# Transposing the attention outputs in the DMA crossbar instead of on TensorE

## The chip, the cores and the metric

The kernel runs on one core of a Trainium2 chip. The metric is the device time of one execution in microseconds. The five engines of the core that matter here are TensorE (PE, with its weight loads listed apart as PEld), VectorE (DVE), ScalarE (ACT), GpSimd (POOL) and SyncE (SP). Each of them works through its own list of instructions in order; they wait for one another on semaphores. Sixteen DMA engines move data; POOL and SP issue the transfers.

## The reference

Four batches of eight heads, 768 rows of 64. Each query row attends to the keys closer than 16 rows and, beside them, to 24 block summaries (the largest key and the mean value of each block of 32). The attention outputs of a batch, heads side by side, are rows of 512 numbers, and these 3072 rows go through two matrix products with a hard-swish between them.

```python
k_sum = k.reshape(B, H, nb, block, D).max(axis=3)
v_sum = v.reshape(B, H, nb, block, D).mean(axis=3)
scores_l = scale * np.matmul(q, k.transpose(0, 1, 3, 2))          # kept where |i - j| < 16
scores_s = scale * np.einsum('bhsd,bhnd->bhsn', q, k_sum) + np.log(block)
a = softmax(concatenate([scores_l_masked, scores_s]))             # over 768 + 24
attn_out = np.matmul(a, np.concatenate([v, v_sum], axis=2))
x = attn_out.transpose(0, 2, 1, 3).reshape(3072, 512)
h = x @ w_in                                                      # 512 x 2048, "GEMM 1"
out = (h * np.clip(h + 3.0, 0.0, 6.0) / 6.0) @ w_out              # 2048 x 512, "GEMM 2"
```

## The kernel before

**Tiling.** A batch has six row tiles T = 0 to 5 of 128 rows each (shifted by 16 rows). Three of them make one token tile: token tile s = 2b for T = 0, 1, 2 of batch b, and s = 2b + 1 for T = 3, 4, 5. There are eight token tiles of 384 rows.

**From attention to GEMM 1.** `scores` (L541) makes the scores on TensorE, ACT takes their exponent (L566) and DVE masks it (L570). `values` (L648) multiplies them with the values on TensorE (L671) into a PSUM pair `S`. `finish` (L687) does the rest for one row tile: DVE takes the reciprocal of the sums (L705) and scales the 128x512 outputs into an SBUF tile `xn` (L709, bf16, rows on partitions). GEMM 1 needs the 512 features on the partitions, so TensorE transposes the tile in four 128x128 matmuls against an identity into a PSUM bank (L724), and ACT or DVE copies the bank into the SBUF tile `x` of the token tile (L726, recorded at the helper's line L463).

**GEMMs.** `f1` (L734) is GEMM 1 for one token tile and 128 of the 2048 inner features: four matmuls of 128x384 (L742), which read all of `x`, then ACT's relu (L747) and DVE's product (L749). The first `f1` of a token tile needs all three of its row tiles. `f2` (L753) is GEMM 2: sixteen matmuls in four groups of four (L762), a copy to an SBUF tile `ot`, and a store issued by SP (L774, two stores L773 and L774 where a tile wraps around).

**Order.** Nothing is scheduled at run time. `ORDER` (L29) is a written list of every operation; each engine executes its operations in the sequence in which their tokens stand there. `F20.0` is the first GEMM 1 product of token tile 2, `G40.5` the store of token tile 4's row tile 0, `v10.3` the fourth operation of `values` for batch 1 beginning at row tile 0, `H2.1` and `H3.0` the halo copies of batches 2 and 3, `u3.4` one of the value-mean copies. A letter after the colon picks the engine of a copy.

**SyncE before the change.** SP issues three kinds of transfer: the stores of `ot`; for batches 2 and 3 the copies of value means into `vaug` (`spread`, L578, 36 KB each, two in a `u` token); and the halos (L437, one of 380 KB in 128-byte pieces, and L439, 32 KB), which copy key-window edges from one set of partitions of `vaug` to another. Eight completion semaphores serve SP's transfers in turn, so one transfer waits for the eighth before it.

**Pools.** There are four `x` tiles, three `xn` tiles, three `ot` tiles, one PSUM bank `o` and two pairs `S`.

The text names only the row tiles of batches 1 to 3; batch 0 is treated apart in the code (`alone`, `banks`).

Of the kernel before, what the change touches and what calls it, by code (L numbers as in the profile page):

```python
# [29 lines left out]
e.1 c.0 K00.0 c.8 z3.0 z1.0 z2.0 K01.0 c.1 Q000.0 K02.0 k00.0 c.2 Q010.0 c.3 c.4 e.0 k00.1 e.3 k00.2:D k00.4 V00.0 V01.0  # L30
k01.0 k01.2:A Q01w2.0 c.6 V02.0 V03.0 q010.0 q000.0 k01.1 k01.4 z0.0 q000.1:A q010.1:A k00.3:A Q01w1.0 I0.0 Q01w0.0 k01.3:A
k03.0 s000.0 k02.0 q030.0 k03.2:A q030.1:D e.2 c.7 I1.0 O0.0 I2.0 q020.0 s010.0 s000.1 s010.1 u00.0 q020.1:A s010.2 k03.1
k02.1 k03.4 k02.4 u00.1:A u00.2:D h010.0:D s000.2 u01.0 s030.0 s030.1 h011.0:D u01.1:D h000.0:D u01.2:D k02.2:A s020.0
s020.1 u02.0 h030.0:D u02.1:D s030.2 h020.0:A s020.2 u03.0 u03.1:D v01.0 v00.0 v00.2 v00.3 v01.2 v01.3 v02.1 I3.0 O2.0 O1.0
v00.1 v01.1 v02.4 v00.4 v00.5 h031.0:A h001.0:A k03.3:A u02.2:A v02.0 v00.6 v00.7:A v01.4 v02.2 v02.3 v01.5 q011.0 v01.6
v02.5 k02.3:A v01.7:D F00.0 v02.6 F00.5 F00.6 q001.0 v02.7:A F00.1 F00.2 q001.1:A F00.3 F00.7 c.5 h021.0:D q031.0 q011.1:A
F00.8 u01.3:D u00.3:D F00.4 F00.9 F01.0 q021.0 F01.3 F01.1 F01.2 q031.1:D F00.15 F00.10 s001.0 q021.1:A F01.4 F01.5 u03.2:D
F00.16 F00.17 s001.1 s001.2 s011.0 F00.11 F00.12 F00.13 F00.14 F01.9 F01.10 c.9 F01.11 F01.6 s011.1 F01.7 s011.2 F01.8
s021.0 F02.9 F02.10 F02.11 s021.1 s021.2 G02.0 s031.0 F02.0 F03.0 F03.3 s031.1 s031.2 F02.1 F03.1 F02.2 F03.2 v04.0 v03.0
v03.1 F03.4 v03.2 F03.5 v04.1 v04.2 F02.3 F02.6 F02.4 F02.5 v03.3 v03.4:A F03.9 v05.0 G02.1 v04.3 z0.1:P z3.1:P K11.0 K12.0  # L40
O3.0 K13.0 z1.1:P K10.0 V12.0 V10.0 V13.0 F03.10 F02.7 v05.1 v05.2 v05.3 v05.4:A F02.8 v04.4:D F03.11 F03.6 F03.7 F10.0
F03.8 F10.3 F10.1 F10.6 F10.4 F10.2 F10.5 F10.9 F10.7 F11.0 F10.8 F10.10 F11.3 F10.11 F11.1 F11.6 F11.2 F11.4 F11.5 F11.7
F11.8 F11.9 F12.6 Q10.0 V11.0 z2.1:P Q12.0 Q13.0 Q11.0 F11.10 F12.7 F11.11 F12.8 F13.0 F12.9 F13.1 F12.10 w12.0 w13.0 F13.2
h121.0:A w11.0 w13.3 w10.0 h100.0:D h130.0:D w10.3 G02.2 F13.6 F13.7 h111.0:D G02.3 F12.0 G02.4:A G01.0 G01.1 G01.2 G01.3
u1.0 h120.0:A F12.1 h101.0:A w10.2:A w13.4:A h131.0:A G01.4:A u1.1:A w12.2:A u1.6:A u1.2:A F12.11 w11.3 F13.8 u1.4:D w11.4:D
w12.3 w10.4:D w12.4:D V22.0 Q20.0 K22.0 K21.0 K20.0 K23.0 Q21.0 Q23.0 Q22.0 V23.0 V21.0 V20.0 w10.1 w10.5:D G00.0 G00.1
F13.9 G00.2 F12.3 G00.3 F13.10 u1.8:A w11.2:A F12.4 h110.0:A w11.1 F12.5 w11.5:D u1.9:D w13.1 w12.1 w12.5:D s100.0 s100.3
s100.1 G00.4:A s110.0 G00.5 s110.1 s110.3 F13.3 G12.0 s120.0 w13.2:A s120.3 s120.1 s110.2 w13.5:D F12.2 F13.11 s110.4 s100.2
# [5 lines left out]
F22.9 F22.10 w21.5:A u2.0 F21.8 w21.3 w21.4:D F22.5 F23.0 Q31.0 Q30.0 V30.0 V32.0 V31.0 V33.0 Q32.0 K33.0 Q33.0 K30.0 K32.0
K31.0 G10.4:A s200.1 u2.1:A F21.9 F21.10 F23.1 F22.11 G11.5 G02.5 u2.2 u2.3 G10.5 H2.0 u2.5 u2.4 w22.1 w22.0 F21.11 F23.3
F23.4 s210.0 G20.0 s210.3 s210.1 F23.2 F23.5 F30.0 G20.1 F23.9 F23.6 w22.5:D F30.1 w22.3 F23.7 w22.4:A F30.2 F23.10 w22.2:D
F23.8 F30.3 G20.2 F30.9 F30.10 s220.0 s220.1 F30.4 s200.2 F23.11 w23.1 F30.11 G20.3 F32.6 F32.0 G20.4:A w23.0 F32.1 w23.5:D
F32.2 F30.5 w23.2:A u3.0 w23.3 s210.2 s220.2 w30.1 G22.0 s220.3 F30.6 G22.1 u3.1:A F32.7 F32.8 w23.4:A F30.7 F30.8 s210.4
s220.4 G22.2 G22.3 G22.4:A s230.0 F31.6 s230.1 s230.3 s230.2 s230.4 F31.3 F31.0 G21.0 F31.4 F31.5 F31.1 v20.0 G21.1 F31.9
F31.10 v20.5 F31.2 v20.1 v20.6 s200.4 F31.11 G21.2 F33.6 F33.7 v20.2 F33.8 F31.7 F31.8 G21.3 F32.9 v20.3 F33.3 G21.4:A  # L60
v20.4:A F33.4 F32.10 u3.4 H2.1 H3.0 G22.5 G20.5 G21.5 v22.0 v25.0 F33.0 w30.0 v22.1 v22.2 F32.11 v25.1 v25.2 F33.1 F33.5
G32.0 F32.3 v20.7 v22.3 F32.4 G32.1 v20.8:A v22.4:A F33.9 F33.2 F32.5 w31.0 F33.10 w30.3 F33.11 F40.0 v23.0 G32.2 F40.9
F40.1 F40.3 w30.4:A F40.10 F40.4 v23.1 F40.2 v23.2 F40.5 F41.3 v23.3 G32.3 v23.4:A F41.4 G32.4:A F40.11 v23.5 F41.5 F40.6
F42.9 G30.0 G30.1 F42.3 v23.6 v23.7 G30.2 w33.0 F42.10 F42.11 w30.5:D w30.2:A F40.7 w31.3 F40.8 w31.2:A F42.4 F42.5 w31.1
F41.0 v25.3 F41.9 F41.1 F41.10 F41.2 F41.11 F42.0 F42.1 w32.1 F42.2 w31.5:D G30.3 F43.6 F43.9 v25.4:A G30.4:A v23.8:D w32.0
w32.3 w33.2:D G31.0 G31.1 w32.4:D F43.7 F43.10 F43.8 w31.4:A s310.0 s310.1 s310.3 G31.2 F43.3 F43.4 w32.5:A F43.5 G31.3
G31.4:A F50.0 F50.1 F42.6 F42.7 F43.11 w32.2:D w33.1 s300.0 s300.3 s300.1 H3.1 G31.5 G32.5 u3.5 u3.3 u3.2 G30.5 F41.6 G41.0
F41.7 F42.8 F50.2 s310.2 F41.8 F50.6 s320.0 F43.0 F50.7 w33.3 w33.5:A F43.1 s320.1 s320.3 F50.8 F43.2 s310.4 w33.4:D s300.2
F52.6 G41.1 F52.7 G41.2 F50.9 F50.10 F50.11 F52.8 F50.3 F50.4 F50.5 s330.0 s330.1 G41.3 G41.4:D s330.2 F52.3 F51.9 F52.0
G42.0 G42.1 F51.10 s330.3 s300.4 s320.2 F52.4 F52.1 F52.5 v30.0 G42.2 G42.3 F53.3 v30.1 v30.5 v30.2 F52.2 F51.11 F51.0  # L70
G42.4:A F51.6 F51.1 s330.4 s320.4 v30.3 G40.0 G40.1 F53.4 v30.4:A v30.6 F51.7 F51.8 F51.2 v35.0 v32.0 v32.1 F53.5 v35.1
v35.2 F52.9 G40.2 F51.3 F53.9 F52.10 F51.4 G40.3 G40.4:A F53.10 F52.11 G41.5 G42.5 G40.5 F51.5 v30.7 F53.6 F53.0 v32.2 v32.3
v32.4:A v30.8:D F53.7 F53.1 G50.0 G50.1 F53.8 F53.2 F53.11 G50.2 F60.3 F60.0 v33.0 F61.9 G50.3 F60.4 F60.1 F60.2 F61.10
F61.11 F60.5 G50.4:A F61.6 F61.0 F61.7 F61.1 v33.5 F61.8 F61.2 v33.1 v33.2 F62.9 F62.10 F62.11 G52.0 G52.1 G52.2 F62.6 G52.3
F62.3 G52.4:D F60.9 v33.3 G51.0 F62.4 F62.7 v33.4:A F62.5 F60.10 F60.11 F62.8 v33.6 G51.1 G51.2 F61.3 F61.4 F61.5 v35.3
F60.6 v35.4:A F63.3 v33.7 F60.7 F63.4 v33.8:A F63.9 F60.8 F63.5 F63.10 F63.11 G51.3 G51.4:A F62.0 F63.6 F62.1 F63.7 F62.2
F63.8 G50.5 G52.5 F70.0 F70.1 G62.0 F70.2 F73.3 F73.4 F73.5 F71.0 F71.1 F71.2 G62.1 F73.9 F63.0 F63.1 F63.2 F70.6 G62.2
G62.3 F70.7 F73.10 F73.11 F71.3 F72.6 F72.7 F71.4 F70.8 G62.4:D F71.5 F70.9 G60.0 F72.8 F70.10 G60.1 F72.0 F72.1 F72.2 G60.2
# [816 lines left out]
```

## Time and profile before

| quantity | value |
|---|---|
| median of 3 runs | 228.15 us (228.09 to 228.6) |
| span of the profiled execution | 226.5 us |
| what lies around the span, against the median | 1.65 us |
| TensorE busy | 216.4 us, 96% of the span |
| DVE, ACT, POOL busy | 158.1, 132.9, 65.3 us |
| matmuls of L724 (transposes) | 96: 84 into `S`, 12 of batch 0 into `h` and `o` |
| copies of `x` out of PSUM | 24: ACT 20, DVE 4 |

The page gives no whole time of the profiled execution beside its span, so the difference to the median stands for what lies around it. Engine times are busy times; PE and PEld overlap. A slice in the second part of the page is 226.5 / 40 = 5.7 us wide.

### The profile page before, as it was taken

Reading aid. Unit: us, or ns where it says so; the run is one execution under the profiler, and the core shown is the slowest. Engines: PE = TensorE matmul, PEld = TensorE weight load, DVE = VectorE, ACT = ScalarE, POOL = GpSimd, SP = SyncE. Lnnn points to the kernel's source line nnn. Section 1 sums busy time; section 2 is a strip of 40 time slices with the busy share of each in tenths; the row PEclk is TensorE's granted clock in tenths of the full one; section 3 lists DMA queues with packets and bytes.
Section 4 is the critical chain, followed back from the end, with each engine's and each line's share of the span. In section 5 each row is a group of like instructions: output and inputs, shape, how many; then the busy total and the mean of one; then the engine's idle time right before and its main releaser. Section 6 shows DMA issues by size and latency. Waiting matters only on the chain.

```text
span 226.5 us, 5318 instructions
## 1 busy us (share of the span) xinstructions
PE 216.4 (96%) x2167; PEld 120.8 (53%) x2167; DVE 158.1 (70%) x329; ACT 132.9 (59%) x274; POOL 65.3 (29%) x75
## 2 busy tenths in 40 slices
PE   6799999999959999999999999999999999999992
PEld 2356765554534565555556555555555555555461
DVE  6667899889797999777789688777654556443211
ACT  2567797679886876858546567873444347435200
POOL 7997871645567648520000000000000000000000
PEclk9999999999997999999999999999999999999999
DMA  5999999999999999999271000331110110020222
GB/s 76 170 150 194 205 206 161 144 127 112 111 108 175 161 190 152 122 115 132 45 174 48 0 3 0 109 72 46 52 46 3 46 46 0 3 93 0 92 72 72
DMA packets 123066, 21.71 MB, mean 96 GB/s; under 512 B 114209, under 2 KB 120097, under 8 KB 123041
## 3 DMA queue, kind: packets, MB, share of 16 engines
q0 software_dynamic: 107920, 13.64, 138.4%
q1 hardware_dynamic: 15120, 7.73, 12.8%
q8 instruction: 17, 0.28, 0.5%
q14 instruction: 9, 0.07, 0.1%
HBM read 27.26 MB, written 6.29 MB: 148 GB/s over the span
## 4 chain that ended last, share of the span: by engine, by line
PE 68%; DMA 12%; POOL 11%; issue 5%; DVE 2%; ACT 1%; POOLq 0%
PE h L742 28%; PE o L762 28%; DMA wout<-in_moe_w_out_dram 7%; DMA qraw<-in_q_dram 5%; PE h L762 5%; POOL vaug L414 3%; PE S L671 3%; PE S L557 2%; PE S L724 2%; POOL qraw L403 2%; POOL win L448 1%; POOL qwide L394 1%; POOL first L374 1%; PE S L605 1%; DVE qT L627 1%
## 5 line engine op out<-in xcount | busy, mean ns | idle before, releaser
L749 DVE SCALAR_TENSOR_TENSOR g<-r,h 128x384 bf16<-128x384 f32 x128 | 67.8, 547 | 40.3 <-ACT r L747 38.6
L742 PE MATMUL h<-x,win 128*128 128x384 bf16 (+1 forms) x536 | 95.4, 319 | 0.2
L747 ACT ACTIVATE r<-h 128x384 f32<-128x384 f32 x128 | 61.4, 491 | 51.0 <-PE h L742 48.9
L762 PE MATMUL o<-wout,g 128*128 128x512 bf16 x336 | 83.7, 384 | 0.0
L742 PEld LDWEIGHTS <-win 128*128 128x128 bf16 x536 | 49.6, 98 | 35.5 <-issue 0.8
L762 PEld LDWEIGHTS <-g 128*128 128x128 bf16 x400 | 37.9, 98 | 36.1 <-issue 1.3
L566 ACT ACTIVATE at<-S 120x768 bf16<-120x768 f32 x32 | 24.9, 813 | 6.2 <-PE S L557 6.2
L414 POOL DMA_DIRECT2D vaug<-in_v_dram x16 | 15.0, 941 | 11.1 <-issue 5.5
L709 DVE TENSOR_TENSOR xn<-S,rc 128x512 bf16<-128x512 f32 (+1 forms) x25 | 16.0, 642 | 0.5
L570 DVE TENSOR_TENSOR at<-at,mask 96x768 bf16<-96x768 bf16 x28 | 14.8, 548 | 1.2 <-ACT at L566 0.9
L463 ACT COPY ot<-o 128x512 f32<-128x512 f32 x18 | 10.6, 588 | 8.4 <-PE o L762 8.4
L463 ACT COPY x<-S 128x512 bf16<-128x512 bf16 x18 | 10.3, 585 | 3.9 <-PE S L724 2.8
L403 POOL DMA_DIRECT2D qraw<-in_q_dram x8 | 10.5, 1313 | 7.3 <-issue 5.2
L557 PEld LDWEIGHTS <-kaug 64*128 64x128 bf16 x384 | 7.3, 97 | 9.1 <-issue 6.4
L403 POOL DMA_DIRECT2D kraw<-in_k_dram x8 | 10.5, 1318 | 4.6 <-issue 2.9
L557 PE MATMUL S<-qT,kaug 64*128 64x64 bf16 x384 | 9.6, 194 | 2.3 <-ACT at L566 0.9
L640 DVE TENSOR_REDUCE red<-kaug 128x24 bf16<-128x768 bf16 x12 | 11.3, 941 | 0.1
L762 PE MATMUL h<-wout,g 128*128 128x512 bf16 (+1 forms) x64 | 10.7, 326 | 0.0
L671 PEld LDWEIGHTS <-at 120*64 120x64 bf16 x360 | 7.0, 111 | 5.2 <-issue 4.5
L848 PE MATMUL o<-idle 128*128 128x512 bf16 x20 | 7.7, 472 | 1.6 <-DVE idle L300 1.6
L671 PE MATMUL S<-vaug,at 120*64 120x65 bf16 x352 | 8.4, 197 | 0.1
L724 PEld LDWEIGHTS <-xn 128*128 128x128 bf16 x96 | 6.9, 98 | 2.8
(100 smaller groups left out, 165.3 us busy)
## 6 DMA issues: line engine op xcount, KB each, us to landing
out_dram<-ot SPq DMA_DIRECT2D x19, 256.0 KB
vaug<-in_v_dram POOLq DMA_DIRECT2D x16, 192.0 KB, 9.1
win<-in_moe_w_in_dram POOLq DMA_DIRECT2D x4, 512.0 KB, 11.0
wout<-in_moe_w_out_dram POOLq DMA_DIRECT2D x4, 512.0 KB, 16.4
kraw<-in_k_dram POOLq DMA_DIRECT2D x8, 192.0 KB, 14.8
qraw<-in_q_dram POOLq DMA_DIRECT2D x8, 192.0 KB, 10.7
first<-in_k_dram POOLq DMA_DIRECT2D x6, 192.0 KB, 8.3
first<-in_q_dram POOLq DMA_DIRECT2D x6, 192.0 KB, 9.6
```

Of the source, the lines that this page charges most:

```text
L403: op("POOL", 1.32, lambda src=src, o=o, hs=hs, ds=ds, rows=rows: nc.gpsimd.dma_start(out=o[rows], in_=src[b, hs].rearrange("h (c r) d -> r ...
L414: op("POOL", 0.95, lambda: nc.gpsimd.dma_start(out=o[BLK:WIN, lo:hi, 0:D], in_=rows[:, lo:hi]), w=[("v", b % 2, c)], prio=prio, dma=1.25, ...
L463: {"ACT": nc.scalar.copy, "DVE": nc.vector.tensor_copy, "POOL": nc.gpsimd.tensor_copy}[eng](o, i)
L557: nc.tensor.matmul(X[p, half].slot[:, j, i * QB:(i + 1) * QB], kaug[p][rows, t], qT[rows, p, t * QB:(t + 1) * QB], start=not masked, stop= ...
L566: op("ACT", act(2 * HALF), lambda a=a, x=x: nc.scalar.activation(a, x.slot[0:KEYS, :, 0:HALF], AF.Exp, scale=scl), r=[x], w=[("at", p, hal ...
L570: op("DVE", 0.57, lambda m=m, half=half: nc.vector.tensor_tensor(m, m, mask[:, low(half):low(half) + HQ].unsqueeze(1).to_broadcast([WIN, 2 ...
L671: nc.tensor.matmul(y, a[:, cols], vaug[b % 2][0:KEYS, h, t, 0:D + 1], start=True, stop=True)
L709: nc.vector.tensor_tensor(o, src[..., 0:D], r.unsqueeze(len(r.shape)).to_broadcast(list(o.shape)), op=ALU.mult)
L742: nc.tensor.matmul(h.slot[:, lo * 128:hi * 128], w_in_sb[:, kt, ft * 128:(ft + 1) * 128], xt[s].slot[:, kt, lo * 128:hi * 128], start=(kt ...
L747: op("ACT", act(HALF), lambda: nc.scalar.activation(r.slot[:], h.slot[:, 0:HALF], AF.Relu, bias=0.5, scale=1.0 / 6.0), r=[h], w=[r], prio= ...
L749: op("DVE", dve(HALF), lambda: nc.vector.scalar_tensor_tensor(gt[s].slot[:, ft], r.slot[:], 1.0, h.slot[:, 0:HALF], op0=ALU.min, op1=ALU.m ...
L762: nc.tensor.matmul(o.slot[:, a:z], gt[s].slot[:, ft, ts * 128:(ts + 1) * 128], w_out_sb[:, ft, a:z], start=(ft == 0), stop=(ft == NFT - 1))
```

## The change

For batches 1 to 3 the four transposing matmuls and the copy out of PSUM are replaced by one DMA from `xn` to `x`, issued by SP, which transposes on the way. That is 18 row tiles: 72 matmuls, 18 copies and 18 uses of a pair `S` go, and 18 transfers of 128 KB come. Batch 0 is unchanged. A fourth `xn` tile is added. The token of the transfer stands in `ORDER` where the token of the matmuls stood; the copy's token is gone; nothing else is moved. The tokens of `v` are renumbered, since two operations have become one.

```diff
-        "xn": [sb([128, d_model], BF16, f"xn{i}") for i in range(3)],
+        "xn": [sb([128, d_model], BF16, f"xn{i}") for i in range(4)],
...
-        Y = Buf(("o", "h") if b == 0 and half == 0 else "S")
+        if b:
+            op("SP", 0.7, lambda: nc.sync.dma_start(out=xt[s].slot[:, :, cols], in_=xn.slot[:], transpose=True),
+               r=[xn] + done, prio=prio + 0.2, dma=0.6, **new)
+            return
+        Y = Buf(("o", "h") if half == 0 else "S")
```

Three places of the order, in the changed kernel's tokens (`v10.3`, `v10.6`, `v12.3`, `v20.3`, `v20.6`, `v22.3`, `v30.6` and `v32.3` are transfers):

```diff
-v10.1 v10.6 v10.2 s130.4 G11.0 G11.1 v12.0 v10.3 v12.1 v12.2 s100.4 w20.0 w20.3 G11.2 v10.4:A v10.7 v10.8:A v12.3 G11.3
-v15.0 v15.1 v15.2 v12.4:A F20.0 G11.4:A F20.1 F20.3 F20.4 F20.6 v13.0 F20.7 F20.2 F20.5 F20.8 F21.0 F22.0 w20.2:A F21.1
+v10.1 v10.5 v10.2 s130.4 G11.0 G11.1 v12.0 v10.3 v12.1 v12.2 s100.4 w20.0 w20.3 G11.2 v10.6 v12.3 G11.3 v15.0 v15.1
+v15.2 F20.0 G11.4:A F20.1 F20.3 F20.4 F20.6 v13.0 F20.7 F20.2 F20.5 F20.8 F21.0 F22.0 w20.2:A F21.1 F22.1 F20.9 v13.1
...
+F31.10 v20.4 F31.2 v20.1 v20.5 s200.4 F31.11 G21.2 F33.6 F33.7 v20.2 F33.8 F31.7 F31.8 G21.3 F32.9 v20.3
+F33.3 G21.4:A F33.4 F32.10 u3.4 H2.1 H3.0 G22.5 G20.5 G21.5 v22.0 v25.0 F33.0 w30.0 v22.1 v22.2 F32.11 v25.1 v25.2
+F33.1 F33.5 G32.0 F32.3 v20.6 v22.3 F32.4 G32.1 F33.9 F33.2 F32.5 w31.0 F33.10 w30.3 F33.11 F40.0 v23.0 G32.2 F40.9
...
+v32.1 F53.5 v35.1 v35.2 F52.9 G40.2 F51.3 F53.9 F52.10 F51.4 G40.3 G40.4:A F53.10 F52.11 G41.5 G42.5 G40.5 F51.5 v30.6
+F53.6 F53.0 v32.2 v32.3 F53.7 F53.1 G50.0 G50.1 F53.8 F53.2 F53.11 G50.2 F60.3 F60.0 v33.0 F61.9 G50.3 F60.4 F60.1
```

More of the change, by code (lines that the diff above doesn't have):

```diff
@@ L29 @@
 ORDER = """
[L30 to L48, printed above, removed]
@@ L49 @@
-F13.4 F13.5 s120.2 G12.1 G12.2 s130.0 s130.1 s130.3 s130.2 s120.4 G12.3 G12.4:A u1.5:A u1.3:A u1.7:A v10.0 G01.5 G12.5 v10.5
-v10.1 v10.6 v10.2 s130.4 G11.0 G11.1 v12.0 v10.3 v12.1 v12.2 s100.4 w20.0 w20.3 G11.2 v10.4:A v10.7 v10.8:A v12.3 G11.3
-v15.0 v15.1 v15.2 v12.4:A F20.0 G11.4:A F20.1 F20.3 F20.4 F20.6 v13.0 F20.7 F20.2 F20.5 F20.8 F21.0 F22.0 w20.2:A F21.1
-F22.1 F20.9 v13.1 v13.2 w20.1 F20.10 w20.5:A G10.0 v13.3 F22.2 v13.4:A w20.4:A G10.1 F21.3 v15.3 v13.5 v13.6 F21.2 F20.11
-F21.6 F22.6 v13.7 G10.2 G10.3 w21.1 w21.0 F21.4 v15.4:A F21.7 F22.7 v13.8:A s200.0 F21.5 F22.8 w21.2:A s200.3 F22.3 F22.4
@@ L54 @@
[L54 to L78, printed above, removed]
@@ L79 @@
-F71.9 F71.10 F70.11 F71.11 F71.6 G60.3 G60.4:A F70.3 F72.9 F70.4 F70.5 F72.10 F71.7 F72.11 F71.8 G61.0 G61.1 F73.0 F73.1
-F73.2 G62.5 G51.5 G61.2 G72.0 F72.3 F72.4 G61.3 F72.5 G61.4:A F73.6 G70.0 G72.1 G72.2 F73.7 F73.8 G71.0 G71.2 G71.4 G71.6
-G72.3 G72.4:D G61.5 G60.5 G72.5 G70.1 G71.7:A G71.8 G70.2 G71.1 G70.3 G70.4:D G70.5 G71.3 G71.5 G71.9 G71.10:A G71.11
+e.1 c.0 K00.0 c.8 z3.0 z1.0 z2.0 K01.0 c.1 Q000.0 K02.0 k00.0 c.2 Q010.0 c.3 c.4 e.0 k00.1 e.3 k00.2:D k00.4 V00.0
+V01.0 k01.0 k01.2:A Q01w2.0 c.6 V02.0 V03.0 q010.0 q000.0 k01.1 k01.4 z0.0 q000.1:A q010.1:A k00.3:A Q01w1.0 I0.0
@@ new lines @@
+Q01w0.0 k01.3:A k03.0 s000.0 k02.0 q030.0 k03.2:A q030.1:D e.2 c.7 I1.0 O0.0 I2.0 q020.0 s010.0 s000.1 s010.1 u00.0
+q020.1:A s010.2 k03.1 k02.1 k03.4 k02.4 u00.1:A u00.2:D h010.0:D s000.2 u01.0 s030.0 s030.1 h011.0:D u01.1:D h000.0:D
+u01.2:D k02.2:A s020.0 s020.1 u02.0 h030.0:D u02.1:D s030.2 h020.0:A s020.2 u03.0 u03.1:D v01.0 v00.0 v00.2 v00.3
+v01.2 v01.3 v02.1 I3.0 O2.0 O1.0 v00.1 v01.1 v02.4 v00.4 v00.5 h031.0:A h001.0:A k03.3:A u02.2:A v02.0 v00.6 v00.7:A
+v01.4 v02.2 v02.3 v01.5 q011.0 v01.6 v02.5 k02.3:A v01.7:D F00.0 v02.6 F00.5 F00.6 q001.0 v02.7:A F00.1 F00.2 q001.1:A
@@ new lines @@
+F00.3 F00.7 c.5 h021.0:D q031.0 q011.1:A F00.8 u01.3:D u00.3:D F00.4 F00.9 F01.0 q021.0 F01.3 F01.1 F01.2 q031.1:D
+F00.15 F00.10 s001.0 q021.1:A F01.4 F01.5 u03.2:D F00.16 F00.17 s001.1 s001.2 s011.0 F00.11 F00.12 F00.13 F00.14 F01.9
+F01.10 c.9 F01.11 F01.6 s011.1 F01.7 s011.2 F01.8 s021.0 F02.9 F02.10 F02.11 s021.1 s021.2 G02.0 s031.0 F02.0 F03.0
+F03.3 s031.1 s031.2 F02.1 F03.1 F02.2 F03.2 v04.0 v03.0 v03.1 F03.4 v03.2 F03.5 v04.1 v04.2 F02.3 F02.6 F02.4 F02.5
+v03.3 v03.4:A F03.9 v05.0 G02.1 v04.3 z0.1:P z3.1:P K11.0 K12.0 O3.0 K13.0 z1.1:P K10.0 V12.0 V10.0 V13.0 F03.10 F02.7
@@ new lines @@
+v05.1 v05.2 v05.3 v05.4:A F02.8 v04.4:D F03.11 F03.6 F03.7 F10.0 F03.8 F10.3 F10.1 F10.6 F10.4 F10.2 F10.5 F10.9 F10.7
+F11.0 F10.8 F10.10 F11.3 F10.11 F11.1 F11.6 F11.2 F11.4 F11.5 F11.7 F11.8 F11.9 F12.6 Q10.0 V11.0 z2.1:P Q12.0 Q13.0
+Q11.0 F11.10 F12.7 F11.11 F12.8 F13.0 F12.9 F13.1 F12.10 w12.0 w13.0 F13.2 h121.0:A w11.0 w13.3 w10.0 h100.0:D
+h130.0:D w10.3 G02.2 F13.6 F13.7 h111.0:D G02.3 F12.0 G02.4:A G01.0 G01.1 G01.2 G01.3 u1.0 h120.0:A F12.1 h101.0:A
+w10.2:A w13.4:A h131.0:A G01.4:A u1.1:A w12.2:A u1.6:A u1.2:A F12.11 w11.3 F13.8 u1.4:D w11.4:D w12.3 w10.4:D w12.4:D
@@ new lines @@
+V22.0 Q20.0 K22.0 K21.0 K20.0 K23.0 Q21.0 Q23.0 Q22.0 V23.0 V21.0 V20.0 w10.1 w10.5:D G00.0 G00.1 F13.9 G00.2 F12.3
+G00.3 F13.10 u1.8:A w11.2:A F12.4 h110.0:A w11.1 F12.5 w11.5:D u1.9:D w13.1 w12.1 w12.5:D s100.0 s100.3 s100.1 G00.4:A
+s110.0 G00.5 s110.1 s110.3 F13.3 G12.0 s120.0 w13.2:A s120.3 s120.1 s110.2 w13.5:D F12.2 F13.11 s110.4 s100.2 F13.4
+F13.5 s120.2 G12.1 G12.2 s130.0 s130.1 s130.3 s130.2 s120.4 G12.3 G12.4:A u1.5:A u1.3:A u1.7:A v10.0 G01.5 G12.5 v10.4
+v10.1 v10.5 v10.2 s130.4 G11.0 G11.1 v12.0 v10.3 v12.1 v12.2 s100.4 w20.0 w20.3 G11.2 v10.6 v12.3 G11.3 v15.0 v15.1
@@ new lines @@
+v15.2 F20.0 G11.4:A F20.1 F20.3 F20.4 F20.6 v13.0 F20.7 F20.2 F20.5 F20.8 F21.0 F22.0 w20.2:A F21.1 F22.1 F20.9 v13.1
+v13.2 w20.1 F20.10 w20.5:A G10.0 v13.3 F22.2 w20.4:A G10.1 F21.3 v15.3 v13.4 v13.5 F21.2 F20.11 F21.6 F22.6 v13.6
+G10.2 G10.3 w21.1 w21.0 F21.4 F21.7 F22.7 s200.0 F21.5 F22.8 w21.2:A s200.3 F22.3 F22.4 F22.9 F22.10 w21.5:A u2.0
+F21.8 w21.3 w21.4:D F22.5 F23.0 Q31.0 Q30.0 V30.0 V32.0 V31.0 V33.0 Q32.0 K33.0 Q33.0 K30.0 K32.0 K31.0 G10.4:A s200.1
+u2.1:A F21.9 F21.10 F23.1 F22.11 G11.5 G02.5 u2.2 u2.3 G10.5 H2.0 u2.5 u2.4 w22.1 w22.0 F21.11 F23.3 F23.4 s210.0
@@ new lines @@
+G20.0 s210.3 s210.1 F23.2 F23.5 F30.0 G20.1 F23.9 F23.6 w22.5:D F30.1 w22.3 F23.7 w22.4:A F30.2 F23.10 w22.2:D F23.8
+F30.3 G20.2 F30.9 F30.10 s220.0 s220.1 F30.4 s200.2 F23.11 w23.1 F30.11 G20.3 F32.6 F32.0 G20.4:A w23.0 F32.1 w23.5:D
+F32.2 F30.5 w23.2:A u3.0 w23.3 s210.2 s220.2 w30.1 G22.0 s220.3 F30.6 G22.1 u3.1:A F32.7 F32.8 w23.4:A F30.7 F30.8
+s210.4 s220.4 G22.2 G22.3 G22.4:A s230.0 F31.6 s230.1 s230.3 s230.2 s230.4 F31.3 F31.0 G21.0 F31.4 F31.5 F31.1 v20.0
+G21.1 F31.9 F31.10 v20.4 F31.2 v20.1 v20.5 s200.4 F31.11 G21.2 F33.6 F33.7 v20.2 F33.8 F31.7 F31.8 G21.3 F32.9 v20.3
@@ new lines @@
+F33.3 G21.4:A F33.4 F32.10 u3.4 H2.1 H3.0 G22.5 G20.5 G21.5 v22.0 v25.0 F33.0 w30.0 v22.1 v22.2 F32.11 v25.1 v25.2
+F33.1 F33.5 G32.0 F32.3 v20.6 v22.3 F32.4 G32.1 F33.9 F33.2 F32.5 w31.0 F33.10 w30.3 F33.11 F40.0 v23.0 G32.2 F40.9
+F40.1 F40.3 w30.4:A F40.10 F40.4 v23.1 F40.2 v23.2 F40.5 F41.3 v23.3 G32.3 F41.4 G32.4:A F40.11 v23.4 F41.5 F40.6
+F42.9 G30.0 G30.1 F42.3 v23.5 v23.6 G30.2 w33.0 F42.10 F42.11 w30.5:D w30.2:A F40.7 w31.3 F40.8 w31.2:A F42.4 F42.5
+w31.1 F41.0 v25.3 F41.9 F41.1 F41.10 F41.2 F41.11 F42.0 F42.1 w32.1 F42.2 w31.5:D G30.3 F43.6 F43.9 G30.4:A w32.0
@@ new lines @@
+w32.3 w33.2:D G31.0 G31.1 w32.4:D F43.7 F43.10 F43.8 w31.4:A s310.0 s310.1 s310.3 G31.2 F43.3 F43.4 w32.5:A F43.5
+G31.3 G31.4:A F50.0 F50.1 F42.6 F42.7 F43.11 w32.2:D w33.1 s300.0 s300.3 s300.1 H3.1 G31.5 G32.5 u3.5 u3.3 u3.2 G30.5
+F41.6 G41.0 F41.7 F42.8 F50.2 s310.2 F41.8 F50.6 s320.0 F43.0 F50.7 w33.3 w33.5:A F43.1 s320.1 s320.3 F50.8 F43.2
+s310.4 w33.4:D s300.2 F52.6 G41.1 F52.7 G41.2 F50.9 F50.10 F50.11 F52.8 F50.3 F50.4 F50.5 s330.0 s330.1 G41.3 G41.4:D
+s330.2 F52.3 F51.9 F52.0 G42.0 G42.1 F51.10 s330.3 s300.4 s320.2 F52.4 F52.1 F52.5 v30.0 G42.2 G42.3 F53.3 v30.1 v30.4
@@ new lines @@
+v30.2 F52.2 F51.11 F51.0 G42.4:A F51.6 F51.1 s330.4 s320.4 v30.3 G40.0 G40.1 F53.4 v30.5 F51.7 F51.8 F51.2 v35.0 v32.0
+v32.1 F53.5 v35.1 v35.2 F52.9 G40.2 F51.3 F53.9 F52.10 F51.4 G40.3 G40.4:A F53.10 F52.11 G41.5 G42.5 G40.5 F51.5 v30.6
+F53.6 F53.0 v32.2 v32.3 F53.7 F53.1 G50.0 G50.1 F53.8 F53.2 F53.11 G50.2 F60.3 F60.0 v33.0 F61.9 G50.3 F60.4 F60.1
+F60.2 F61.10 F61.11 F60.5 G50.4:A F61.6 F61.0 F61.7 F61.1 v33.4 F61.8 F61.2 v33.1 v33.2 F62.9 F62.10 F62.11 G52.0
+G52.1 G52.2 F62.6 G52.3 F62.3 G52.4:D F60.9 v33.3 G51.0 F62.4 F62.7 F62.5 F60.10 F60.11 F62.8 v33.5 G51.1 G51.2 F61.3
@@ new lines @@
+F61.4 F61.5 v35.3 F60.6 F63.3 v33.6 F60.7 F63.4 F63.9 F60.8 F63.5 F63.10 F63.11 G51.3 G51.4:A F62.0 F63.6 F62.1 F63.7
+F62.2 F63.8 G50.5 G52.5 F70.0 F70.1 G62.0 F70.2 F73.3 F73.4 F73.5 F71.0 F71.1 F71.2 G62.1 F73.9 F63.0 F63.1 F63.2
+F70.6 G62.2 G62.3 F70.7 F73.10 F73.11 F71.3 F72.6 F72.7 F71.4 F70.8 G62.4:D F71.5 F70.9 G60.0 F72.8 F70.10 G60.1 F72.0
+F72.1 F72.2 G60.2 F71.9 F71.10 F70.11 F71.11 F71.6 G60.3 G60.4:A F70.3 F72.9 F70.4 F70.5 F72.10 F71.7 F72.11 F71.8
+G61.0 G61.1 F73.0 F73.1 F73.2 G62.5 G51.5 G61.2 G72.0 F72.3 F72.4 G61.3 F72.5 G61.4:A F73.6 G70.0 G72.1 G72.2 F73.7
@@ L82 @@
+F73.8 G71.0 G71.2 G71.4 G71.6 G72.3 G72.4:D G61.5 G60.5 G72.5 G70.1 G71.7:A G71.8 G70.2 G71.1 G70.3 G70.4:D G70.5
+G71.3 G71.5 G71.9 G71.10:A G71.11
 """
```

## The prediction

> **What bounds the kernel now.** I read the page first: the shares, the slices and the chain.
>
> ```profile
> span 226.5 us, 5318 instructions
> PE 216.4 (96%) x2167; PEld 120.8 (53%) x2167; DVE 158.1 (70%) x329; ACT 132.9 (59%) x274; POOL 65.3 (29%) x75
> ...
> PE   6799999999959999999999999999999999999992
> ...
> DMA  5999999999999999999271000331110110020222
> ```
>
> TensorE is the bound. The one weak slice (62 to 68 us) is a wait for batch 1's scores; from 74 us to the last copy the chain in order of time is TensorE alone. So every TensorE microsecond removed after 74 us comes off the end, and every wait of TensorE there is added to it. The DMA row is as important: the DMA engines are full until about 107 us, nearly idle after.
>
> Then the chain by time, around the first GEMM 1 product of token tile 2 (F20.0):
>
> ```profile
> 77.86 0.45 PE S L724 x8
> 78.31 0.86 PE o L762 x4
> 79.17 0.37 PE S L671 x15
> 79.54 2.06 PE h L742 x12
> ```
>
> The transposes of row tiles 1 and 2 are followed by only 1.23 us of other work (0.86 + 0.37) before F20.0 reads their result. Next, what SP does around 110 us:
>
> ```profile
> 110.23 1.60 SPq L578 DMA_DIRECT2D vaug<-vs  x2
> 111.94 0.64 SPq L439 DMA_DIRECT2D vaug<-vaug  x1
> 112.82 0.64 SPq L437 DMA_DIRECT2D vaug<-vaug  x1
> 113.55 4.61 SPq L774 DMA_DIRECT2D out_dram<-ot  x3
> ```
>
> The columns are start, duration, engine and line. Behind the 380 KB halo of L437 the next store takes 2.91 us to issue (the longest of its group; its data had been ready since 109.8): the halo's 3040 packets back up into SP. The same follows the other such halo (100.18 us: the next issue takes 5.92 us).
>
> Last, what a gap costs in clock:
>
> ```profile
> 62.90:66.20 3.30, 1.05 (x36) 0.87 (x36) 3.23 (x6) 2.45 (x5) 2.62 (x2) 1.00 6.43 105
> 67.20:70.60 3.40, 3.40 (x32) 1.40 (x31) 3.37 (x9) 2.28 (x6) 2.32 (x3) 0.51 5.05 147
> ```
>
> PE works 1.05 of 3.30 us, and then gets a clock of 0.51 for 3.4 us: 1.7 us lost after one such gap.
>
> I keep the times of this trace below ("reached at") and count each wait as pushing all that is behind it.
>
> **Removed.** The x8 row is 0.45 us, 0.056 per matmul; 72 matmuls of L724 make 4.05 us, all on the chain: **-4.0**. The 18 copies out of PSUM (585 ns on ACT, 418 on DVE) and the uses of S are beside TensorE's work and worth nothing. No value product, scale or reciprocal changes.
>
> **Price of one transposing transfer.** The trace has none. What it shows of SP's transfers, from issue to the last landing mark: an undisturbed store of 256 KB 2.0 us (168.05 to 170.05); the same with full DMA engines 4.95 us (74.38 to 79.33) and 5.13 (79.82 to 84.95), first packet after 2.9 and 2.7; a 32 KB halo 1.98 us (111.94 to 113.92); the 380 KB halo 5.56 (112.82 to 118.38). The latency undisturbed is thus 2.0 us. For the data, the low end is the store: three in a row land 0.64 us apart for 256 KB, so 0.4 for 128 KB with something for small rows. The high end is the whole excess of the halo over the short one, 3.6 us. I take 1.3 us, the halo's 3.6 us for 348 KB scaled to 128 KB, as it is the only row from SBUF to SBUF with small pieces. SP's own issue takes 0.33 (store) to 0.99 us (value copies); I take 0.5.
>
> [...]
>
> **Wait 1, F20.0.** DVE ends the scales at 75.47, 76.06 and 77.64 (L709). On SP the three transfers stand behind the store of 74.38, whose packets end at 78.9. In line after it, 1.3 us each, the third is through at 82.8 and marked at 83.2. Without its transposes TensorE reaches F20.0 at 79.54 - 0.67 = 78.87. Wait: **+4.3**. Low end 2.9 (first packet 2.9 us after 77.7, 0.8 us of data, mark at 81.8); high end 11.3 with 3.6 us each. Behind it **+1.7** of half clock (0 if the gap falls unluckily little into one stretch).
>
> **Wait 2, v25.0 and F40.0.** v20.3 stands on SP ahead of u3.4, H2.1, H3.0 and three stores, and can't be issued before its scale ends at 114.53; in the trace before, SP had done u3.4 to H3.0 by 113.5. Now: v20.3 114.6 to 115.1, two value copies to 116.8, H2.1 lands at 118.8, as v25.0 is reached (118.75), so no wait or up to 0.5 there. H3.0 at 117.5 lands at 123.1 and holds the stores: 118.2 to 121.1, then 121.6 and 122.0; v20.6 and v22.3 issue at 122.1 to 123.1. Their data come after halo and stores (three stores had landed 1.9 us after the halo: 125.0), 2.6 us for both: 127.6. F40.0 is reached at 123.2 - 0.45 = 122.8 (the two transposes at 121.60 are gone). **+4.8** for both places; low end 2.9 by store-like data, high end 9.5. **+1.7** of half clock again, 0 to 1.7.
>
> **Wait 3, F60.3.** v30.6 stands behind the store G40.5, issued at 168.05, though its scale ends at 160.5; v32.3's ends at 167.60. Both issue by 169.4; the store lands at 170.05, they 2.6 us later, at 172.65. F60.3 is reached at 171.7 - 0.45 = 171.3. **+1.4**, from 0 to 6.0.
>
> **What hides the rest.** Token tile 3: last scale 85.7, F30.0 reached at 95.4. Token tile 5: 130.2 against 142. Token tile 7: 185.5 against 189.9; 4.4 us hide 2.0 + 1.3. If a transfer's data took over 2.4 us, tile 7 would wait too. DVE's scale of row tile 3 (82.9) reuses the first xn, free at about 80.6: 2.3 us of cover. Stores stuck behind transfers: G11.5 goes from 79.8 to about 86 and the next copies into `ot` are at 92.7 and 103.0; the store of 175.93 goes to 186, with three `ot` tiles and the buffer wanted again at 198. Both are free. POOL's queue isn't passed.
>
> **Sum.** -4.0 + 4.3 + 1.7 + 4.8 + 1.7 + 1.4 = +9.9. The profiled span of 226.5 lies 1.65 under the median of 228.15, and I keep that distance: 236.4 span, **238.0 us**. With all low ends -4.0 + 2.9 + 2.9 = +1.8, 229.9.
>
> **Rivals.**
>
> 1. *The transfer itself is slow*: 3.6 us of data each, the halo's price. Then 11.3 at F20.0; at F30.0 three more follow the scale of 83.56, 83.56 + 2.0 + 10.8 = 96.4 and 1.0 of wait; 9.5 at F40.0; 6.0 at F60.3; 185.5 + 5.6 against 189.9, 1.2, at F70.0; three times 1.7 of clock. +34.1 - 4.0 = +30: **258 us**. For it: the halo is SBUF to SBUF, like this. Against: the halo has 3040 packets for 380 KB, more than 128 KB in rows need.
> 2. *SP's queue stays clear*: the order on SP does not hold H3.0 back far enough, because token tile 2's delay also gives SP time. Only F20.0 waits, and 0.8 + 0.4 remain of waits 2 and 3: -4.0 + 4.3 + 1.7 + 1.2 = +3.2, **231.4 us**. Against: v20.3 waits for a scale that is pushed back by the same delay.
> 3. *Faster*: a transposing transfer lands 2.0 us after SP reaches it, whatever else the DMA engines hold. Then F20.0 waits 77.7 + 2.0 - 78.87 = 0.8, F40.0 123.0 + 2.0 - 122.8 = 2.2 at most, F60.3 nothing, with gaps too short for the clock: -4.0 + 3.0 = -1.0, **227.1 us**. It decides as soon as the waits sum to less than 4.0. Against: both stores issued in that stretch took 5 us. That the change does nothing isn't possible: the matmuls go.
>
> **Chances.** Forecast 0.50 (its own range 232 to 246), slow transfer 0.20, clear queue 0.20, faster rival 0.10, of which 0.02 falls within 0.2%, about what a measurement of this kernel can tell from no change. So faster 0.08, same 0.02, slower 0.90. The range reaches down to the low ends, 229.5, and up to 259, the slow transfer's time, leaving out the faster rival and the upper half of the slow one.
>
> **What would show it.** In the profile after: no L724 into S; TensorE idle before F20.0 for about 4 us, released by a DMA into `x`; a half clock right behind; a second such idle stretch before F40.0, with SP's halo issue later than the first transfer of token tile 4; a short one before F60.3; nothing before F30.0, F50.0 and F70.0. The prediction is wrong if the landing under full DMA engines differs much from 5 us, if SP's issue of one transfer takes several us (each then delays all stores and halos), or if waits fall in other places.

## The result and the profile after

The changed kernel takes 245.41 us (median of 4, 243.16 to 246.92) against 228.12 us: a ratio of 1.0747 with a 95% interval of 1.0656 to 1.0837. The profiled execution took 246.92 us, the slowest of the four, with a span of 245.2, so the account of the spans below explains some 1.5 us more than the median lost.

The page after, first its shares and slices:

```profile
span 245.2 us, 5166 instructions
PE 214.4 (87%) x2065; PEld 118.3 (48%) x2095; DVE 157.5 (64%) x327; ACT 125.0 (51%) x258; POOL 65.6 (27%) x75
...
PE   7998999999595099999897199999999799999993
PEclk9999999999999659999999559999999999999999
DMA  6999999999999999999914712023032032020023
```

TensorE still has nearly the same busy time, but no longer all of the span: there are two holes in its row, at slices 13 and 14 and at 22 and 23, and within each the granted clock falls to 0.50 and stays there behind it (slices 14 and 15, 23 and 24; the windows below have the figures). The busy time falls only from 216.4 to 214.4 us although 72 matmuls are gone, since others ran at that clock.

The waits of TensorE, from the view of waits (who waited for whom; us in total, times, the longest):

```profile
PE h L748 <- DMA x<-xn: 16.4, 2, 9.6
PE S L673 <- DMA vaug<-vs: 1.3, 2, 0.7
PE h L748 <- issue: 1.3, 1, 1.3
```

And the same in the order of time, TensorE's timeline at F20.0 and at F40.0, where the brackets hold the idle time before and its releaser, and SP's timeline around the second:

```profile
76.37 0.44 PE L673 MATMUL S<-vaug,at 120*64 120x65 bf16 x16
86.40 4.00 PE L748 MATMUL h<-x,win 128*128 128x384 bf16 x12 [9.59 <-DMA x<-xn]
...
140.03 1.44 PE L748 MATMUL h<-x,win 128*128 128x384 bf16 x4 [6.80 <-DMA x<-xn]
```

```profile
126.90 1.23 SPq L722 DMA_TRANSPOSE x<-xn  x1
128.23 1.69 SPq L580 DMA_DIRECT2D vaug<-vs  x2
129.97 0.65 SPq L441 DMA_DIRECT2D vaug<-vaug  x1
130.87 0.64 SPq L439 DMA_DIRECT2D vaug<-vaug  x1
131.60 4.10 SPq L780 DMA_DIRECT2D out_dram<-ot  x3
135.75 2.72 SPq L722 DMA_TRANSPOSE x<-xn  x2
```

TensorE stands 9.59 us before token tile 2 and 6.80 us before token tile 4. In the second case the first transfer, the halo and the stores stand on SP in the written order, and the two transfers that F40.0 lacks are issued only at 135.75, after the 4.10 us of stores held up behind the halo. Twelve matmuls of GEMM 1 took 4.00 us after the first wait, and 2.06 us in the trace before: the half clock.

The windows show it. The columns are the stretch, its length, busy time and count of PE, PEld, DVE, ACT and POOL, the granted clock, the DMA share and GB/s:

```profile
81.50:86.40 4.90, 0.00 (x1) 0.03 (x1) 0.00 (x0) 0.00 (x0) 0.00 (x0) 0.50 3.07 111
86.40:91.70 5.30, 5.30 (x46) 2.77 (x47) 1.81 (x5) 2.08 (x5) 0.02 (x1) 0.50 1.90 33
140.00:146.30 6.30, 5.93 (x46) 3.02 (x48) 1.23 (x3) 1.30 (x3) 0.00 (x0) 0.50 0.11 23
```

The account of the spans, 226.5 to 245.2, +18.7 us. Up to the first product of batch 1's values the kernel after is 1.9 us ahead (71.51 against 73.40 us): its profiled execution had no half-clock stretch near 67 us, where the one before had 3.4 us. Then -4.0 for the matmuls; +9.6 before F20.0; +1.3 before v20.0 (value copies, L673 in the list of waits); +6.8 before F40.0; +1.3 before F60.3 (put down to "issue" in the list; the third transfer of token tile 6 lands at 191.12, just before 191.21); +0.3 for one wait of L768 behind F40.0; half of 5.3 and of 6.3 us for the clock, +5.8. Together +19.2, which is 0.5 us more than the spans differ; that is not accounted for.

What one transfer costs, from the marks of landing: SP needs 1.19 to 1.44 us to issue it in this trace. The first of token tile 4, with the DMA engines nearly free (a DMA share of 0.26 in that stretch), is issued at 126.90 and lands at 129.35, 2.45 us; of the eighteen, nine land in 2.4 to 2.9 us. The three of token tile 2 are issued at 73.99, 75.35 and 76.70 and land at 82.73, 84.92 and 86.26: 8.7 to 9.6 us, at a DMA share of 2.63 in 74.0 to 86.3.

### The profile page after: what moved, and what is told of

Same layout as the page of the kernel before. It is cut to its first block, busy times and chain, and to the rows that moved or that the text cites. A ratio compares the mean times of both kernels' runs of the same rounds, so it can differ in the third digit from the quotient of the medians.

```text
span 245.2 us, 5166 instructions
## 1 busy us (share of the span) xinstructions
PE 214.4 (87%) x2065; PEld 118.3 (48%) x2095; DVE 157.5 (64%) x327; ACT 125.0 (51%) x258; POOL 65.6 (27%) x75
## 4 chain that ended last, share of the span: by engine, by line
PE 47%; DMA 24%; POOL 12%; issue 6%; SPq 5%; ACT 3%; DVE 2%; DVEq 0%; POOLq 0%
PE h L748 22%; PE o L768 18%; DMA wout<-in_moe_w_out_dram 6%; DMA x<-xn 6%; DMA kraw<-in_k_dram 5%; PE h L768 4%; DMA qraw<-in_q_dram 4%; SPq L580 3%; POOL vaug L416 3%; PE S L673 2%; DMA vaug<-vs 2%; POOL qraw L405 2%; ACT at L568 2%; POOL win L450 1%; POOL qwide L396 1%
## 5 line engine op out<-in xcount | busy, mean ns | idle before, releaser
L748 PE MATMUL h<-x,win 128*128 128x384 bf16 (+1 forms) x536 | 98.4, 328 | 18.2 <-DMA x<-xn 16.4
L768 PE MATMUL o<-wout,g 128*128 128x512 bf16 x311 | 79.5, 382 | 2.2 <-DVE g L755 0.6
L748 PEld LDWEIGHTS <-win 128*128 128x128 bf16 x536 | 50.8, 100 | 57.4 <-issue 16.6
L768 PEld LDWEIGHTS <-g 128*128 128x128 bf16 x400 | 38.2, 98 | 37.3 <-issue 0.8
L707 DVE RECIPROCAL rc<-S 128x8 f32<-128x8 f32 (+1 forms) x25 | 4.9, 198 | 12.6 <-PE S L673 12.3
L673 PEld LDWEIGHTS <-at 120*64 120x64 bf16 x360 | 7.9, 119 | 7.2 <-issue 6.6
L768 PE MATMUL h<-wout,g 128*128 128x256 bf16 (+1 forms) x63 | 10.7, 325 | 0.1
L673 PE MATMUL S<-vaug,at 120*64 120x65 bf16 x352 | 9.6, 206 | 1.3 <-DMA vaug<-vs 1.3
L629 DVE STREAM_TRANSPOSE qT<-qraw 128x768 bf16<-128x768 bf16 x8 | 7.7, 969 | 0.1
```

What stands on the lines that cost most here:

```text
L673: nc.tensor.matmul(y, a[:, cols], vaug[b % 2][0:KEYS, h, t, 0:D + 1], start=True, stop=True)
L748: nc.tensor.matmul(h.slot[:, lo * 128:hi * 128], w_in_sb[:, kt, ft * 128:(ft + 1) * 128], xt[s].slot[:, kt, lo * 128:hi * 128], start=(kt ...
L768: nc.tensor.matmul(o.slot[:, a:z], gt[s].slot[:, ft, ts * 128:(ts + 1) * 128], w_out_sb[:, ft, a:z], start=(ft == 0), stop=(ft == NFT - 1))
```

## The experiments

Theory: the transfer in itself is short; the time goes where its reader comes soon, because the DMA engines are full (F20.0) or because SP's written order puts a halo and stores ahead (F40.0, F60.3), and then in the clock. Rival: transposing in the crossbar is slow in itself. A second rival, after the first results: every use of the transposing transfer gives back what TensorE saves. In the runs below the lines of the transfer, of GEMM 1's matmul and of the halo stand one lower (L721, L747, L438) than in the changed kernel, except in e9_orderonly. The runs were made on three chips, each with its own runs of the kernel before: 227.54 us for e1, e2, e3 and e4, 227.69 for e4b, e5, e8 and e9, 228.16 for e7. Across chips, ratios to the kernel before are compared.

**e3_plain: the same transfers without transposing.**

```diff
-op("SP", 0.7, lambda: nc.sync.dma_start(out=xt[s].slot[:, :, cols], in_=xn.slot[:], transpose=True),
+op("SP", 0.7, lambda: nc.sync.dma_start(out=xt[s].slot[:, :, cols], in_=xn.slot[:].rearrange("p (k c) -> p k c", k=NP)),
```

> The 18 transfers copy xn to x without transposing (this part of the computation is left out), same bytes, same order on SP. Theory (full DMA engines and SP's queue make the waits, not the crossbar): SP's issue falls from 1.25 to about 0.4 us, but the wait before F20.0 stays at 5 us or more, as the stores there take 5 us, and 4 us or more stay before F40.0 behind the halo: 236 to 242 us. Rival (the crossbar is the cost): the wait before F20.0 falls under 3 us, that before F40.0 under 3 us: 233 us or less.

Measured in one execution: 242.28 us, just above the expected 236 to 242. TensorE's waits in this run:

```profile
PE h L747 <- DMA x<-xn: 13.0, 3, 6.7
PE S L672 <- DMA vaug<-vs: 1.1, 1, 1.1
```

6.7 us before F20.0, 5.6 before F40.0, 0.7 before F60.3. SP's issue is 0.59 to 0.78 us, about half of the transposing one, and the landing with free engines 2.26 to 2.40 us, against 2.4 to 2.5. With full engines token tile 2's copies land 7.1 to 7.8 us after issue. So a plain copy in the same place leaves most of each wait, 6.7 of 9.6 us and 5.6 of 6.8; what transposing adds is 2.9 and 1.2 us. The longer issue, some 0.6 us for each of three transfers in line, would be an estimated 1.8 us of that; the run doesn't separate the rest. The rival falls: the first transfer of token tile 4 lands in 2.45 us transposing and in 2.37 us plain, but the issue on SP is twice as long.

**e4_lateloads and e4b_lateloads: the DMA engines without the loads of batch 2.** The first form only moved the twelve loads from ahead of w10.1 to behind F20.2 in the list, with the tokens of w20 behind them, and gave each of them a dependence on F20.2:

```diff
-w12.3 w10.4:D w12.4:D V22.0 Q20.0 K22.0 K21.0 K20.0 K23.0 Q21.0 Q23.0 Q22.0 V23.0 V21.0 V20.0 w10.1
+w12.3 w10.4:D w12.4:D w10.1
...
+F20.7 F20.2 V22.0 Q20.0 K22.0 K21.0 K20.0 K23.0 Q21.0 Q23.0 Q22.0 V23.0 V21.0 V20.0
...
+o.deps.add(made["F20.2"])
```

> The twelve loads of batch 2 are held until the first product of token tile 2 is made, so the DMA engines are empty of them when token tile 2's three transfers run; the transforms of batch 2's first keys are moved behind them. What is looked at is only that stretch; the whole time will be worse, since batch 2 starts late. Theory (full engines make the landing long): each of the three lands 2.5 to 3.5 us after its issue instead of 8.7 to 9.6, and the wait before F20.0 falls from 9.6 to 2 or 3 us. Rival (transposing is slow in itself): they still land 7 us or more after issue and the wait stays above 7 us.

Measured in one execution: 248.87 us, the three landings 8.9 to 9.2 us after issue, 8.87 us of wait. It doesn't test the theory: the dependence was known to the list's planner alone, POOL saw no reason to wait, and its loads of batch 2 ran at 59 to 78 us as ever. But it shows that moving w20 alone does not shorten the landing, and so it is what the second form has to be compared with. The second form has the same order and made POOL read the product, in a new operation y.0:

```diff
+op("POOL", 0.1, lambda: nc.gpsimd.tensor_copy(flag[:], gt[2].slot[:, 0, 0:2]), r=[("g", 2, 0)], w=["flag"])
...
+F20.7 F20.2 y.0 V22.0 Q20.0 K22.0 K21.0 K20.0 K23.0 Q21.0 Q23.0 Q22.0 V23.0 V21.0 V20.0
```

> As in the run e4_lateloads, but held by an instruction of POOL that reads token tile 2's first product ahead of the twelve loads of batch 2, so that they really start after F20.0. Looked at is only the landing of token tile 2's three transfers. Theory (full engines): 2.5 to 3.5 us after issue instead of 9, wait before F20.0 2 to 3 us. Rival: 7 us or more after issue. The whole time is worse, 250 us or more.

Measured in one execution: 258.3 us, with 20.6 us of waiting for batch 2's late keys, as meant. POOL's and TensorE's timelines at the place that counts:

```profile
81.51 0.19 POOL L857 COPY flag<-g 128x2 bf16<-128x2 bf16 x1 [27.43 <-DVE g L754]
```

```profile
75.88 0.44 PE L672 MATMUL S<-vaug,at 120*64 120x65 bf16 x16
79.53 2.11 PE L747 MATMUL h<-x,win 128*128 128x384 bf16 x12 [3.20 <-DMA x<-xn]
```

POOL is held until 81.5, the DMA share in 72 to 80 us is 0.44, against 2.69 in the changed kernel (a sum of packet times over the engines, which can pass 1), and the three transfers land 3.86, 3.25 and 2.47 us after issue, the first a little later than expected. The wait is 3.2 us and GEMM 1 runs on at full clock (2.11 us for twelve matmuls). Against e4_lateloads, with 8.87 us, the loads cost 5.7 us of the wait, against the changed kernel 6.4 of its 9.6; what is left is latency and SP's 1.3 to 2.0 us for each issue, one after the other.

**e2_sporder: only SP's order.**

```diff
-... G21.3 F32.9 v20.3 F33.3 G21.4:A F33.4 F32.10 u3.4 H2.1 H3.0 G22.5 G20.5 G21.5 v22.0 ... v20.6 v22.3 F32.4
+... G21.3 F32.9 u3.4 H2.1 v20.3 F33.3 G21.4:A F33.4 F32.10 v22.0 ... v20.6 v22.3 H3.0 G22.5 G20.5 G21.5 F32.4
-... G41.5 G42.5 G40.5 F51.5 v30.6 F53.6 F53.0 v32.2 v32.3 F53.7
+... G41.5 G42.5 F51.5 v30.6 F53.6 F53.0 v32.2 v32.3 G40.5 F53.7
```

> All 18 transfers as in the changed kernel; only SP's own order is altered: u3.4 and H2.1 before v20.3, H3.0 and the stores G22.5, G20.5, G21.5 behind v22.3, the store G40.5 behind v32.3. Theory (the waits at F40.0 and F60.3 come from what stands ahead on SP): the wait before F40.0 falls from 6.8 us to under 1 and the one before F60.3 from 1.3 to 0, the second half-clock stretch (3.1 us) goes, the 9.6 us before F20.0 stay: about 234 us. Rival (the transfer itself takes too long for 2.8 us of cover): 4 us or more remain before F40.0 and the time stays above 241 us.

Measured: 235.78 us, a little above the expected 234, ratio 1.0374 (1.0306 to 1.0443). TensorE's waits, and SP's timeline to lay beside the one above:

```profile
PE h L747 <- DMA x<-xn: 8.4, 1, 8.4
PE S L672 <- DMA vaug<-vs: 1.6, 2, 1.0
```

```profile
127.86 5.27 SPq L721 DMA_TRANSPOSE x<-xn  x3
133.36 0.66 SPq L438 DMA_DIRECT2D vaug<-vaug  x1
134.12 4.09 SPq L779 DMA_DIRECT2D out_dram<-ot  x3
```

The three transfers now go out ahead of the halo, and of the waits for x only the one before F20.0 is left, in this run 8.4 us. The ratio falls from 1.0747 to 1.0374, some 8.5 us of 228, and most of it lay in the order of one queue and in the clock behind it. A half-clock stretch does remain in that part: behind the 1.6 us of waits for value copies the clock is 0.50 from 124.12 to 127.53 us, which the expectation did not have.

**e5_no2: token tile 2 back on TensorE.**

```diff
-if b:
+if (b, half) in [(1, 1), (2, 0), (2, 1), (3, 0), (3, 1)]:
```

> As the changed kernel, but token tile 2 is transposed on TensorE (fifteen row tiles by DMA), SP's order not altered otherwise. Theory: the 9.6 us before F20.0 and the half clock behind it (2.7 us) go, 0.7 us of matmuls come back, the wait of about 7 us before F40.0 with 3 us of half clock stays: 233 to 236 us. Rival (the wait before F40.0 is only a result of the earlier delay): under 230 us.

Measured in one execution: 235.28 us, as expected. TensorE waits for x twice:

```profile
PE h L747 <- DMA x<-xn: 8.0, 2, 7.0
```

The wait before F40.0 is 7.00 us without the one before F20.0, so it is no echo of that; e2_sporder shows that it is SP's order. The wait before F60.3 is 0.96.

**e1_odd: only token tiles 3, 5 and 7.**

```diff
-if b:
+if (b, half) in [(1, 1), (2, 1), (3, 1)]:
```

> Only token tiles 3, 5 and 7 use the transposing DMA (nine row tiles); token tiles 2, 4 and 6 are transposed on TensorE as before. Theory (the transfer costs nothing where its reader comes late enough): no wait of TensorE before F30.0, F50.0 and F70.0, 36 matmuls of 0.056 us less, 2.0 us: 226.1 us against 228.1. Rival (SP's long issues and the extra transfers delay stores, halos and loads everywhere): waits of 1 us or more remain in other places and the time is 228 us or more.

Measured: 228.52 us, ratio 1.0043 (1.0003 to 1.0083): no gain, against my expectation of 2.0 us; the time is the one that the rival gave, 228 us or more. There is no wait before F30.0, F50.0 or F70.0, as the theory said; but the profile shows others, of TensorE for the value copies and for GEMM 1's product, and of DVE for the keys of batch 3:

```profile
PE h L747 <- DVE g L754: 1.2, 2, 0.9
PE S L672 <- DMA vaug<-vs: 0.8, 1, 0.8
```

```profile
DVE kaug L624 <- DMA kraw<-in_k_dram: 1.7, 1, 1.7
```

The kernel before has none of the three: DVE's wait for the keys stands right ahead of the late product at 121 us. I read it as token tile 3's transfers (6.9 to 9.0 us to landing) taking room from batch 3's loads; the next runs test what follows from that.

**e8_b23 and e9_orderonly: the transfers only after the loads, and the order alone.**

```diff
-if b:
+if (b, half) in [(2, 0), (2, 1), (3, 0), (3, 1)]:
...
-u2.2 u2.3 G10.5 H2.0 u2.5 u2.4
+u2.2 u2.3 u2.5 u2.4 H2.0 G10.5
```

with e2_sporder's order; e9_orderonly has the same order and no transposing transfer.

> Only batches 2 and 3 use the transposing DMA (twelve row tiles, all after the loads are done); batch 1 is transposed on TensorE as before. SP's order as in the run e2_sporder, and u2.4 and u2.5 ahead of H2.0. Theory (transfers cost nothing where the DMA engines are free and SP's queue is clear; in the loaded stretch they hold up the loads): no wait for x anywhere, 48 matmuls of 0.056 us less: 2.7 us faster than before, about 225 us. Rival (removed TensorE work is taken up by other waits anyway, as in e1_odd): within 0.5 us of before.

> The kernel before with the order on SP of e8_b23 and no transposing DMA. Theory: the order of SP alone is worth nothing here, the same time as before within 0.5 us. Rival (the value means ahead of the halo end a hidden wait): 1 us or more faster.

Measured: e8_b23 224.91 us, ratio 0.9841 (0.9791 to 0.9892); e9_orderonly 227.09 us, ratio 0.9959 (0.9922 to 0.9997). The order alone gives some 0.4%, a little more than I expected. Between the two lie 0.0118 of 227.7, 2.7 us, which is what 48 matmuls of 0.056 us make; each ratio is known to about half a per cent. The slices of e8_b23:

```profile
span 221.3 us, 5203 instructions
PE   7999999999959999999999999999999999999993
DMA  5999999999999999999414820330711123020212
```

No hole is left behind slice 12, and its list of waits has none for x, vaug or kraw. All twelve transfers are issued after 114 us, and they land 2.4 to 4.2 us later. This version is faster than both kernels; against the kernel before the gain is 1.1 to 2.1%.

**e7_with3: token tile 3 added to e8_b23.**

```diff
-if (b, half) in [(2, 0), (2, 1), (3, 0), (3, 1)]:
+if (b, half) in [(1, 1), (2, 0), (2, 1), (3, 0), (3, 1)]:
```

> The run e8_b23 with token tile 3's three row tiles put on the transposing DMA too; they are issued while the DMA engines are full of batch 3's loads. Theory (there the transfers hold up the loads, as in e1_odd, where DVE waited 1.67 us for the keys of batch 3): the 0.7 us of matmuls saved are given back, a ratio to before no better than 0.984 and more likely 0.985 to 0.99. Rival (TensorE's saving counts there too): 0.981 or less.

Measured: 224.83 us, ratio 0.9864 (0.9819 to 0.9910). Inconclusive: it is no better than e8_b23's 0.9841, as the theory had it, but the intervals overlap, and its profile shows no wait for the keys of batch 3. Nor does e5_no2's, which has the same three transfers. That the wait of 1.67 us in e1_odd comes from the transfers is therefore not shown; the 0.8 us for the value copies is gone with the new order on SP.

## Why the prediction was right, and where it was not

**Direction and mechanism.** Slower, 245.4 us in a range of 229.5 to 259.0; forecast 238.0. The loss of 17.3 us is larger than the forecast 9.9 but comes in the main from the three places that were named and from the clock behind two of them.

**Removed, -4.0.** Right as far as it was measured: e8_b23 against e9_orderonly gives 2.7 us for 48 of the 72 matmuls, which leaves nothing that stands out for the copies and the uses of S. For the 24 matmuls of batch 1 no run shows it.

**Price of one transfer.** The latency of 2.0 plus data of 1.3 us with free engines made 3.3; it is 2.45. SP's issue, taken as 0.5 us between 0.33 and 0.99, is 1.19 to 1.44, outside the bounds. The packets of token tile 4's first transfer, 512 of 256 bytes, took 0.8 us (128.10 to 128.87) against the 1.3 us for the data.

**Wait 1, 4.3 forecast, 9.6 measured.** The mechanism was right and its size was off. The failed step is "1.3 us each, the third is through at 82.8": with full engines the packets ran from 77.9 to 85.5, 2.5 us for each transfer. I had used a price from nearly free engines for the data and put the load into the latency alone; three times 1.2 us is 3.6 of the 5.3 us that were missing. In e4b_lateloads, without the loads, the wait is 3.2 us.

**Half clock, 1.7 twice forecast, 2.65 and 3.15 measured.** I took the one stretch of 3.4 us of the trace before. In the changed kernel the clock is 0.50 for 10.24 us at each of the two long waits (81.47 to 91.71 and 136.09 to 146.32), three times the 3.41 us of the one before, and 5.3 and 6.3 us of it fell behind the waits. How a gap has to lie or how short it has to be for the clock to stay up, on which the zero in the forecast and the third rival counted, was my estimate and is not shown: behind the 3.2 us of wait in e4b_lateloads GEMM 1 ran at full clock, behind 1.6 us of waits in e2_sporder the clock was 0.50 for 3.41 us.

**Wait 2, 4.8 forecast, 6.8 measured.** Right in its place and its cause: e5_no2 shows it alone, 7.0 us, and e2_sporder takes it away by SP's order. The step that failed is "can't be issued before its scale ends at 114.53". In `ORDER` the scale of the other row tile (v20.5, which v20.6 waits for) stands ahead of v20.2, the one that v20.3 waits for. DVE's timeline before, and the same second scale after:

```profile
113.89 0.64 DVE L709 TENSOR_TENSOR xn<-S,rc 128x512 bf16<-128x512 f32 x1
...
115.84 0.68 DVE L709 TENSOR_TENSOR xn<-S,rc 128x512 bf16<-128x512 f32 x1
```

```profile
126.18 0.68 DVE L711 TENSOR_TENSOR xn<-S,rc 128x512 bf16<-128x512 f32 x1
```

v20.3's own scale ended at 116.52 there, 2.0 us later than I read, and that is the whole difference; in the changed kernel it ended at 126.86, and v20.3 was issued at 126.90. The rest of the sum came out by luck: from the end of the scale to the last landing it has 13.1 us and the trace 13.0 (126.86 to 139.90), but the pair for F40.0 took SP 2.7 us instead of 1.0, and the last landing came 1.4 us behind it instead of 4.5. The forecast of little or nothing before v25.0 held.

**Wait 3, 1.4 forecast, 1.3 measured.** The place and the cause are right: it is gone in e2_sporder. The size is luck in part: SP took 2.7 us for the two issues (187.17 to 189.90), forecast as 1.0, and the last landing came 1.2 us behind them (191.12), forecast as 3.3.

**What hides the rest.** Right: no wait for x before F30.0, F50.0 and F70.0. Not foreseen was the wait of 1.3 us before v20.0 for value copies held behind a halo: the first copy behind the halo of 108.10 took SP 6.95 us to issue, and the last two landed at 122.17 and 122.95, just before TensorE went on.

**The rivals.** The slow transfer, at 0.20, is refuted by e3_plain and by 2.45 us. A clear queue on SP is refuted by the changed kernel itself: H3.0 was issued at 130.87, 4.0 us behind v20.3, and the wait of 6.8 us followed, though token tile 2 was late. A landing 2.0 us after SP, whatever the engines hold, is refuted by the 8.7 to 9.6 us.

## What to carry to other kernels

Before work is moved from a saturated engine to a DMA, look up how soon its reader comes and what the DMA engines do in that stretch: the same transfer landed in 2.45 us and in 9.6 us, and a gain came only where the transfers had cover, free engines and a clear queue. Read the issuing queue's list as a program of its own: TensorE waited 7 us here for transfers written behind a halo and three stores, and a new order took that wait away. Look up which operation a transfer waits for by its place in the order: two equal lines of the profile were taken for one another here, and that was 2.0 us. Then take the change by parts: all eighteen tiles cost 7.5%, the twelve after the loads, with the queue in order, gained 1.6%, some 0.4% of it by the order alone.
